# A four-layer attention/gated-MLP kernel: the first chunk's q and k from unpermuted weights, its softmax divided after the sum with v

## The chip, the cores and the metric

The kernel runs on one core of one Trainium2 chip. The time is what the device takes for one execution, in microseconds; of several runs the median counts. Engines are named as in the profile: PE is TensorE's matmul stream and PEld its weight loads, DVE is VectorE, ACT is ScalarE, POOL is GpSimd, SP is SyncE, whose queue issues all DMAs here.

## What is computed

Two kinds of layers alternate, A B A B, on 2048 tokens of width 576, each with a layer norm in front and a residual behind. A is attention with 32 heads of width 18, where each token looks at itself and at the tokens 2, 4, ... 14 before it. B is a gated product with 4608 hidden columns.

```python
def _A_ref(x, wqkv, wo):
    q, k, v = split_heads(x @ wqkv)                      # H = 32, Dh = 18
    off = jnp.arange(8) * 2
    idx = pos[:, None] - off[None, :]
    ...
    logits = jnp.einsum("bhsd,bhswd->bhsw", q, kg) * scale
    logits = jnp.where(mask[None, None, :, :], logits, -1e9)
    attn = _softmax(logits, axis=-1)
    o = jnp.einsum("bhsw,bhswd->bhsd", attn, vg)
    return o_joined @ wo

def _B_ref(x, w_gate, w_up, w_down):
    h = (x @ w_gate) * (x @ w_up)
    return h @ w_down

x = A_x
x = x + _A_ref(_layernorm(x, axis=-1), A_wqkv, A_wo)
x = x + _B_ref(_layernorm(x, axis=-1), B_w_gate, B_w_up, B_w_down)
x = x + _A_ref(_layernorm(x, axis=-1), A_wqkv, A_wo)
x = x + _B_ref(_layernorm(x, axis=-1), B_w_gate, B_w_up, B_w_down)
```

Both A layers use the same weights, and so do both B layers. `B_x` is not used.

## The kernel before

The tokens are cut into 16 tiles of 128. A chunk is one or two tiles: the first four chunks of the first layer pair are one tile each, the others two. For each chunk `attention` (L439) runs a layer A and `glu` (L768) a layer B. The list `seq` (L876) takes eight tiles through the first pair, then through the second, then the other eight.

No engine's order is written by hand. Every step is handed to `Plan.op` (L34) with its engine, a cost in nanoseconds, the keys that it reads and writes, and a priority; `Plan.run` (L70) then plays the steps against clocks of its own and emits them in that order, so each engine's queue is fixed when the program is built. `after=` adds an order without a data dependency, `hold`/`free` hand out PSUM banks, and `pair`/`need` the two "units" (a gate bank `pg` and an up bank `pu` each) that gate/up matmuls and projections share. While TensorE would idle before the first gate/up matmul, `warm` (L757) fills in matmuls of the identity.

All activations are kept transposed, features on partitions. For attention the 576 features of q, k and v are stored in the order (d, h), so that one partition block of 32 is one d for all heads: four full blocks of 128 and a tail of 64. The weights lie in DRAM as (h, d); so `setup_a` (L272) loads the raw rows into `wraw`, four blocks of 128 rows and the last 64 rows twice (both partition halves), 3456 bytes a row, and `setup_b` (L284) permutes their columns into `wqkv`: for each row block k, 512 columns of q and of v on VectorE (L305), of k on ScalarE (L307), and the last 192 columns on GpSimd (L303) or, for the last block, on VectorE. `wraw` lies in a pool that is given back (`swap`, L323), and the products' buffers are allocated in its place. SP's queue holds: two tiles of x, the six loads of `wraw`, two more tiles of x, eight loads of the output weights, then gate, up and down weights in slices.

The first chunk (`fast`, j = 0) is special. `head` (L353) normalizes the tile (statistics on VectorE, rstd by Ln and Exp on ScalarE, scaling on ScalarE L375, transposition on TensorE L386, eviction on ScalarE L389). `project` (L458) then runs, for each row block k, all fourteen output blocks of q, k, v (L469), as weights arrive. Four VectorE products of q with k shifted by two window places each (L580) are summed over d by matmuls with the selector `Esel` (L596). Softmax: mask (L616), maximum (L636), subtraction (L619), Exp on ScalarE (L659), sum and reciprocal (L664, L667), scaling (L670). The weights, one row for each head and quarter of the tokens, are spread to all partitions by matmuls with `Bsel` (L680) and evicted by ScalarE and VectorE (L522, L520). Eight VectorE products with shifted v (L714) are summed by identity matmuls (L718, L719), evicted (L734, L736), and `tail_fast` (L394) runs the output projection with the residual as an identity matmul (L400, L405), the second normalization (L407 to L423), its transposition (L429) and eviction (L431), which the first gate/up matmul (L793) waits for. Later chunks run the same steps in the shadow of the gate/up/down matmuls; chunk 1's and chunk 2's attention is partly ahead of L793 in TensorE's queue. The last 14 columns of k and v of a chunk are kept in `halo_k`, `halo_v` for the next (L562, L453, L526).

Of the kernel before, what the change touches and what calls it, by code (L numbers as in the profile page):

```python
# [7 lines left out]
FP32 = mybir.dt.float32  # L8
# [12 lines left out]
class Plan:  # L21
# [38 lines left out]

    def also(self, o, keys):

        for k in keys:
            for p in list(self.wr.get(k, ())) + list(self.rd.get(k, ())):
                if p is not o and p not in o.deps and p not in o.order:
                    o.deps.add(p)
                    p.succ.append(o)
                    o.n += 1

    def run(self, slots):  # L70
# [5 lines left out]
        while cand:  # L76
# [36 lines left out]
            if o.eng == "PE" and self.warm is not None:  # L113
                if o is self.cool:
                    self.warm = None
                else:
                    self.warm(min(44, int(max(0, t - clock["PE"] - 100) / 100)))
# [22 lines left out]
def kernel(  # L140
# [58 lines left out]
    Bsel = sb("Bsel", [P, 4, 4, 32])  # L199
    xf = [sb(f"xf{i}", [P, NST, D], FP32) for i in range(NXS)]  # L200
# [7 lines left out]
    zs_t = sb("zs", [P, CH // 4], FP32)  # L208
    xn_ = [[sb(f"xn{a}{i}", [P, KT * P]) for i in range(2)] for a in range(2)]
# [19 lines left out]
    startup_pool = tc.tile_pool(name="startup", bufs=1)  # L229
    sp = startup_pool.__enter__()  # L230
    wraw = sp.tile([P, KT, 3 * D], BF16, name="wraw")
    late = {}

# [29 lines left out]
    def load_x(t0, nst):  # L263
        b, i0 = (t0 // 2) % 2, t0 % 2
        if t0 == 2:
            op("POOL", 80, lambda: nc.gpsimd.memset(xb[b][0:1, i0, 0:2], 0.0), r=["wq3_0"], w=[f"xb{b}_{i0}"])
# [5 lines left out]
    def setup_a():  # L272
# [6 lines left out]
        for k in range(KF):  # L279
            op("SP", 500, dma(wraw[:, k, :], A_wqkv[k * P:(k + 1) * P, :]), w=[f"wraw{k}"], nbytes=P * 3 * D * 2, prio=1)  # L280
        for r_ in (0, TL):
            op("SP", 500, dma(wraw[r_:r_ + TL, KF, :], A_wqkv[KF * P:D, :]), w=[f"wrawt{r_}"], nbytes=TL * 3 * D * 2, prio=1)

    def setup_b():  # L284
        def mk_zero():
            for t_ in qT_ + kT_ + vT_:
                nc.gpsimd.memset(t_[TL:P, KF, :], 0.0)
            for t_ in halo_k + halo_v:
                nc.gpsimd.memset(t_[:], 0.0)
        op("POOL", 1500, mk_zero, w=[f"{x}{t}{i}" for x in "qkv" for t in (4, "H") for i in range(2)] + [f"halo{x}{i}" for x in "kv" for i in range(n_al)])  # L290
        for k in range(KT):
            for t3 in (0, 1, 2, 3):
                if t3 < 3:
                    src = wraw[:, k, t3 * D:(t3 + 1) * D].rearrange("p (h d) -> p d h", h=H)[:, 0:16, :]
                    dst = wqkv[:, k, t3 * 512:(t3 + 1) * 512].rearrange("p (d h) -> p d h", h=H)
                    cost = (615, 1080)
                else:
                    src = wraw[:, k, :].rearrange("p (t h d) -> p t d h", t=3, h=H)[:, :, 16:18, :]
                    dst = wqkv[:, k, 3 * 512:3 * D].rearrange("p (t d h) -> p t d h", t=3, h=H)
                    cost = (280, 500)  # L300
                rk = [f"wraw{k}"] if k < KF else ["wrawt0", f"wrawt{TL}"]
                if t3 == 3 and k < KF:
                    op("POOL", 700, lambda dst=dst, src=src: nc.gpsimd.tensor_copy(dst, src), r=rk, w=[f"wq{t3}_{k}"], prio=2)  # L303
                elif t3 != 1:
                    op("DVE", cost[0], lambda dst=dst, src=src: nc.vector.tensor_copy(dst, src), r=rk, w=[f"wq{t3}_{k}"], prio=2)  # L305
                else:
                    op("ACT", cost[1], lambda dst=dst, src=src: nc.scalar.copy(dst, src), r=rk, w=[f"wq{t3}_{k}"], prio=2)  # L307

        def mk_sel():
            nc.gpsimd.memset(Esel[:], 0.0)  # L310
# [10 lines left out]
        op("POOL", 5000, mk_sel, w=["sel"])  # L321

        def swap():  # L323
            startup_pool.__exit__(None, None, None)
            rot = ctx.enter_context(tc.tile_pool(name="rot", bufs=1))
            late["prod"] = [rot.tile([P, 2, KT, CH], BF16, name=f"prod{i}") for i in range(2)]
            late["s1"] = rot.tile([P, 8 * CH], BF16, name="s1")
            late["Lt"] = rot.tile([P, 2 * CH], FP32, name="Lt")
            late["a_c"] = late["s1"][:, 0:2 * CH]
            late["ab"] = rot.tile([P, 4, 2 * CH], BF16, name="ab")  # L330
        op("POOL", 0, swap, r=[f"wq{t}_{k}" for t in range(4) for k in range(KT)],
           w=["prod0", "prod1", "s10", "s11", "s12", "s13", "Lt", "ab"])

# [9 lines left out]
    def setup_glu():  # L343
        fw = F // FS
        for s in range(FS):
            fs = slice(s * fw, (s + 1) * fw)
            for nm, dst, src in (("wg", wg, B_w_gate), ("wu", wu, B_w_up)):
                op("SP", 500, dma(dst[:, :, fs], src[0:KF * P, fs].rearrange("(k p) f -> p k f", p=P)),
                   w=[f"{nm}{s}"], nbytes=P * KF * fw * 2, prio=4 + s, after=marks["x"])
# [3 lines left out]
    def head(src, keys, nst, dst, key, prio, ab, on_pe, mg, first=None, then=None):  # L353

        mv, st, rstd, nmr, xn = mv_[ab], st_[ab], rstd_[ab], nmr_[ab], xn_[ab]
        for i in range(nst):
# [573 lines left out]
```

## Time and profile before

| | |
|---|---|
| Runs | 1080.16, 1080.99, 1083.73 us; median 1080.99 |
| The profiled execution | 1079.86 us, its span 1078.1 us |
| Granted TensorE clock | 1.000 of full speed |
| TensorE busy up to 32 us, and 400 to 600 us | 26.1 of 32, and 199.4 of 200 |
| DMA, mean of the span | 136 GB/s (146 MB) |
| First gate/up matmul (L793) starts | 32.66 us |
| Last qkv weight copied by GpSimd / VectorE | 11.1 / 13.4 us |

The span runs from the first to the last instruction; the time of the execution holds what lies around it as well. A busy TensorE in the table includes the filler matmuls. The profile is one execution, and a name such as `pg` stands for all its buffers. In the chain of waits each piece is what the next one waited for, so a stretch of it is a stretch of the kernel's time, while a busy engine beside it is not.

### The profile page before, as it was taken

How to read it: one execution, taken by the hardware profiler on the slowest of the kernel's cores; microseconds unless marked ns; L12 is line 12 of the kernel's file. 1: busy time of each engine (PE TensorE's matmuls, PEld its weight loads, DVE VectorE, ACT ScalarE, POOL GpSimd, SP SyncE). 2: the span in 40 equal slices, each digit the busy share in tenths (PEclk: the TensorE clock that was granted, in tenths of full speed). 3: DMA queues.
4: the chain of work that ended last, by engine and by line, in shares of the span. 5: the costliest groups of instructions: out<-in, count | busy, mean ns of one | idle time of the engine just before them, and what ended most of it. 6: DMA issues, size and time to landing. Idle time of an engine off the chain costs nothing.

```text
span 1078.1 us, 25413 instructions
## 1 busy us (share of the span) xinstructions
PE 1063.8 (99%) x10797; PEld 787.7 (73%) x10797; DVE 755.1 (70%) x1345; ACT 369.4 (34%) x756; POOL 8.8 (1%) x39
## 2 busy tenths in 40 slices
PE   8999999999999999999999999999999999999998
PEld 6788877777777777777777777777777777777775
DVE  7677987786959776685967778595876869472222
ACT  6544254332421544131242332423243332212121
POOL 3000000000000000000000000000000000000000
PEclk9999999999999999999999999999999999999999
DMA  9973774645263644435363734536353543534331
GB/s 278 342 208 92 208 175 122 169 105 138 79 169 105 153 115 108 126 112 150 109 170 97 162 93 121 134 84 170 89 153 91 127 116 106 157 112 112 101 110 56
DMA packets 155089, 146.16 MB, mean 136 GB/s; under 512 B 43104, under 2 KB 152672, under 8 KB 154976
## 3 DMA queue, kind: packets, MB, share of 16 engines
q1 hardware_dynamic: 154976, 144.55, 49.6%
q8 instruction: 84, 1.38, 0.5%
q14 instruction: 29, 0.24, 0.1%
HBM read 125.11 MB, written 10.88 MB: 126 GB/s over the span
## 4 chain that ended last, share of the span: by engine, by line
PE 95%; DMA 2%; DVE 2%; SPq 1%; issue 1%; ACT 0%; DVEq 0%; ACTq 0%
PE pg L793 24%; PE pu L793 23%; PE acc L832 23%; PE pg L804 7%; PE pg L469 5%; PE pu L469 4%; PE pa L746 4%; PE acct L834 3%; DMA wraw<-in_A_wqkv_dram 1%; DMA a_dram<-s 1%; DMA ab<-a_dram 1%; DVE h L816 0%; SPq L257 0%; DVE prod L714 0%; PE pa L680 0%
## 5 line engine op out<-in xcount | busy, mean ns | idle before, releaser
L816 DVE TENSOR_TENSOR h<-pu,g_sb 128x512 bf16<-128x512 f32 x288 | 196.3, 686 | 200.8 <-ACT g_sb L815 149.6
L815 ACT CAST g_sb<-pg 128x512 bf16<-128x512 f32 x288 | 168.2, 585 | 476.6 <-PE pu L804 391.3
L832 PE MATMUL acc<-wd,h 128*128 128x512 bf16 x1152 | 306.3, 380 | 0.0
L793 PE MATMUL pg<-xnT_B,wg 128*128 128x256 bf16 (+1 forms) x2592 | 300.8, 261 | 0.8 <-ACT xnT_B L431 0.8
L793 PE MATMUL pu<-xnT_B,wu 128*128 128x256 bf16 (+1 forms) x2592 | 299.3, 261 | 0.0
L793 PEld LDWEIGHTS <-wg 128*128 128x128 bf16 x2592 | 212.5, 98 | 61.2 <-issue 26.2
L793 PEld LDWEIGHTS <-wu 128*128 128x128 bf16 x2592 | 230.9, 98 | 23.3
L834 PE MATMUL acct<-wd,h 128*128 128x64 bf16 x1152 | 222.0, 193 | 0.0
L832 PEld LDWEIGHTS <-h 128*128 128x128 bf16 x1152 | 112.7, 98 | 117.9
L714 DVE TENSOR_TENSOR prod<-vT,ab 128x1280 bf16<-128x1280 bf16 (+1 forms) x127 | 92.9, 741 | 66.5 <-DMA ab<-a_dram 66.4
L469 PEld LDWEIGHTS <-wqkv 128*128 128x128 bf16 (+1 forms) x1260 | 95.4, 97 | 30.3 <-issue 16.1
L834 PEld LDWEIGHTS <-h 128*128 128x128 bf16 x1152 | 112.9, 98 | 2.2
L580 DVE TENSOR_TENSOR prod<-qT,kT 128x2560 bf16<-128x2560 bf16 (+1 forms) x72 | 95.5, 1331 | 1.0 <-ACT kT L522 0.4
L731 DVE TENSOR_TENSOR oT<-oT,prod 128x1280 bf16<-128x1280 bf16 (+1 forms) x119 | 90.8, 763 | 3.0
L804 PE MATMUL pu<-xnT_B,wgu_t 64*128 64x256 bf16 (+1 forms) x648 | 88.1, 260 | 0.0
L804 PE MATMUL pg<-xnT_B,wgu_t 64*128 64x256 bf16 (+1 forms) x648 | 88.0, 260 | 0.0
L469 PE MATMUL pg<-xnT_A,wqkv 128*128 128x256 bf16 (+3 forms) x650 | 79.7, 260 | 1.5 <-issue 0.9
L469 PE MATMUL pu<-xnT_A,wqkv 128*128 128x256 bf16 (+3 forms) x610 | 76.5, 262 | 2.6 <-DVE h L816 2.1
L804 PEld LDWEIGHTS <-wgu_t 64*128 64x128 bf16 x1296 | 47.0, 94 | 32.5 <-issue 27.8
L746 PE MATMUL pa<-wo_p,oT 128*128 128x288 bf16 x310 | 48.2, 286 | 0.1
L375 ACT ACTIVATE xn<-xf,nmr,rstd 128x576 bf16<-128x576 f32 x47 | 40.7, 866 | 8.8 <-DVE nmr L367 8.8
L584 DVE TENSOR_TENSOR prod<-prod 128x1024 bf16<-128x1024 bf16 (+1 forms) x64 | 41.1, 643 | 0.8
(117 smaller groups left out, 563.1 us busy)
## 6 DMA issues: line engine op xcount, KB each, us to landing
wd<-in_B_w_down_dram SPq DMA_DIRECT2D x324, 288.0 KB, 3.3
s_dram<-s SPq DMA_DIRECT2D x13, 512.0 KB, 3.7
prod<-s_dram SPq DMA_DIRECT2D x52, 128.0 KB, 2.9
ab<-a_dram SPq DMA_DIRECT2D x52, 128.0 KB, 2.7
wg<-in_B_w_gate_dram SPq DMA_DIRECT2D x6, 768.0 KB, 9.8
wu<-in_B_w_up_dram SPq DMA_DIRECT2D x6, 768.0 KB, 10.4
out_dram<-ob SPq DMA_DIRECT2D x8, 288.0 KB, 2.6
wraw<-in_A_wqkv_dram SPq DMA_DIRECT2D x4, 432.0 KB, 5.0
```

The costliest lines, as they stand in the source:

```text
L469: nc.tensor.matmul(bank(p_, u)[0:m, e * n:(e + 1) * n], lhsT=wqkv[r_, k, c0:c0 + m], rhs=xnT_A[r_, k, 0:n], start=start, stop=stop, skip_g ...
L580: nc.vector.tensor_tensor(late["prod"][p_ % 2][:, :, :, 0:n], q2, k2, op=ALU.mult)
L584: nc.vector.tensor_tensor(prod[:, :, 0:4:2, 0:n], prod[:, :, 0:4:2, 0:n], prod[:, :, 1:4:2, 0:n], op=ALU.add)
L714: nc.vector.tensor_tensor(js(dst), js(vT[:, :, o0:o0 + n]), abw, op=ALU.mult)
L731: op("DVE", 60 + 3 * n, lambda i_=i_: nc.vector.tensor_tensor(oT[:, :, 0:n], oT[:, :, 0:n], late["prod"][i_ % 2][:, 0, :, 0:n], op=ALU.add ...
L746: nc.tensor.matmul(b()[:, 0:HD], lhsT=oT[:, t, i * P:(i + 1) * P], rhs=wo_p[:, t, hh * HD:(hh + 1) * HD], start=(t == 0), stop=(t == KT - 1))
L793: nc.tensor.matmul(pt[:, e * n:(e + 1) * n], lhsT=w_[:, k, ft * P:(ft + 1) * P], rhs=xT[:, k, 0:n], start=(first and k == 0 and e == 0), s ...
L804: nc.tensor.matmul(ps[:, e * n:(e + 1) * n], lhsT=wgu_t[r_, ft * P:(ft + 1) * P], rhs=xT[r_, KF, 0:n], start=(first and e == 0), stop=not ...
L815: op("ACT", 590, lambda: nc.scalar.copy(g_sb[gs][:, 0:ul], pg[use["slot"]][:, 0:ul]), r=[f"wg_{j}_{u}"], w=[f"g{gs}"], prio=0)
L816: op("DVE", 690, lambda: nc.vector.tensor_tensor(hb[hs][:, 0:ul], pu[use["slot"]][:, 0:ul], g_sb[gs][:, 0:ul], op=ALU.mult), r=[f"wu_{j}_{ ...
L832: nc.tensor.matmul(acc[i][:], lhsT=lhs, rhs=wt[:, e % 2, 0:512], start=(ft == 0), stop=(ft == NFT - 1))
L834: nc.tensor.matmul(acct[:, i * TL:(i + 1) * TL], lhsT=lhs, rhs=wt[:, e % 2, 512:D], start=(ft == 0 and i == 0), stop=(ft == NFT - 1), skip ...
```

## The change

- **Loads.** `wraw` is no tile of its own any more: its row blocks are the upper columns (2304 to 4031) of the `wu` and `wg` tiles, whose weights for these columns come later (their loads now also wait for the last reader of the raw weights). The columns of q and k (1152) are loaded first, in six loads, then those of v (576) in six more. Since nothing is given back, `swap` goes, and the products' buffers are allocated at the start.
- **Projection of the first chunk.** q and k are projected from the raw weights, block by block as these arrive (`natural`, `natural_tails`), so that they come out in the order (h, d). The selector that sums over d is a new one, `Nsel`, which sums features of one head in that order. v is projected from the permuted weights behind it, and k's last 14 columns, which chunk 1 needs in the order (d, h), are projected again from the permuted weights (`halo_mm`, from a copy `xh` of the last 14 tokens).
- **Permuting.** The copies into `wqkv` are dealt out anew: VectorE takes q, one block of v and one of k; ScalarE four of v, one of k; GpSimd all blocks of 192 columns and three of k's 512. They are behind the first chunk's own steps where `behind` says so.
- **Softmax of the first chunk.** Exp writes bf16 weights that are not divided; they are spread at once. The sums' reciprocals are split into two bf16 parts (`zh`), spread by eight small matmuls into `zb`, and multiply the summed products as these are evicted (on VectorE, where before ScalarE and VectorE copied).
- **The rest.** The first tile is scaled on VectorE; the output projection of the first chunk is in two steps (four blocks, then the tail); its transposed result is evicted by ScalarE (three blocks) and VectorE (two); the statistics and the transposed tile of one-tile chunks have a slot each; some priorities, orders and evictions of chunks 1 to 3 differ; the filler matmuls write a free unit's bank instead of `pa`.

```diff
@@ tiles
+    Nsel = sb("Nsel", [P, KT, 32])
+    xh = sb("xh", [P, KT, HALO])
+    zh = sb("zh", [P, 2, P // 4])
+    zb = sb("zb", [P, P], FP32)
-    startup_pool = tc.tile_pool(name="startup", bufs=1)
-    sp = startup_pool.__enter__()
-    wraw = sp.tile([P, KT, 3 * D], BF16, name="wraw")
+    wr0 = F // 2
+    wraw = [(wu[:, k] if k < KF else wg[:, 0])[:, wr0:wr0 + 3 * D] for k in range(KT)]
...
@@ setup_a
-        for k in range(KF):
-            op("SP", 500, dma(wraw[:, k, :], A_wqkv[k * P:(k + 1) * P, :]), ...)
-        for r_ in (0, TL):
-            op("SP", 500, dma(wraw[r_:r_ + TL, KF, :], A_wqkv[KF * P:D, :]), ...)
+        for c, cols in enumerate((slice(0, 2 * D), slice(2 * D, 3 * D))):
+            for k in range(KT):
+                for r_, key in zip(rows_[k], rk_[c][k]):
+                    m = r_.stop - r_.start
+                    op("SP", 500, dma(wraw[k][r_, cols], A_wqkv[k * P:k * P + m, cols]), w=[key], ...)
+            if c == 0:
+                load_x(1, 1)
...
@@ setup_b
+        for k in range(KT):
+            perm("DVE", 0, k)
+        for k in range(KT):
+            perm("ACT" if k else "DVE", 2, k)
+        for k in range(KT):
+            perm("POOL", 3, k)
+        for k in range(KT):
+            perm(("DVE", "ACT")[k] if k < 2 else "POOL", 1, k)
...
@@ head
+            if fast:
+                op("DVE", 600, apply_d, r=[keys[i - io], f"mv{ab}{i}", f"rstd{ab}{i}"], w=[f"xn{ab}{i}"], prio=0)
...
@@ attention, first chunk
+            def natural(k):
+                for e in range(KF):
+                    for p_ in range(2):
+                        nc.tensor.matmul(bank(p_, ua)[:, e * n:(e + 1) * n], lhsT=wraw[k][:, p_ * D + e * P:p_ * D + (e + 1) * P], rhs=xA[:, k, :], ...)
+                for p_ in range(2):
+                    nc.tensor.matmul(bq()[:, p_ * n:(p_ + 1) * n], lhsT=wraw[k][:, 512 + p_ * 512:640 + p_ * 512], rhs=xA[:, k, :], ...)
...
+            def vfull(p_, e, c0):
+                for k in range(KF):
+                    nc.tensor.matmul(bank(p_, uv)[:, e * n:(e + 1) * n], lhsT=wqkv[:, k, c0:c0 + P], rhs=xA[:, k, :], ...)
...
+            op("ACT", 250, lambda: nc.scalar.copy(xh[:], xA[:, :, n - HALO:n]), r=xk, w=["xh"], prio=prio)
...
@@ attention, chunk 1
+            def halo_mm(e):
+                for k in range(KF):
+                    nc.tensor.matmul(bh()[:, e * HALO:(e + 1) * HALO], lhsT=wqkv[:, k, parts[e]:parts[e] + P], rhs=xh[:, k, :], ...)
...
@@ attention, sum over d
-                        nc.tensor.matmul(pav[32 * jj:32 * jj + 32, 2 * p_:2 * p_ + 2, :], lhsT=Esel[:],
+                        nc.tensor.matmul(pav[32 * jj:32 * jj + 32, 2 * p_:2 * p_ + 2, :], lhsT=Nsel[:, i_] if fast else Esel[:],
...
@@ attention, softmax
+        if fast:
+            marks["exp"] = op("ACT", 400, lambda: nc.scalar.activation(late["a_c"][:, 0:W * sq], late["Lt"][:, 0:W * sq], ACT.Exp), ...)
...
+                if fast and j0:
+                    pl.behind(marks["perms"]["ACT", 1, 1], ev)
+                    pl.behind(marks["perms"]["DVE", 1, 0], lastp)
...
+                op("DVE", 590, lambda: nc.vector.tensor_reduce(out=zs_t[:, 0:sq], in_=wv(late["a_c"]).rearrange("p w s -> p s w"), op=ALU.add, axis=AX.X), ...)
+                def invert():
+                    nc.vector.reciprocal(zs_t[:, 0:sq], zs_t[:, 0:sq])
+                    nc.vector.tensor_copy(zh[:, 0], zs_t[:, 0:sq])
+                    nc.vector.tensor_tensor(zh[:, 1], zs_t[:, 0:sq], zh[:, 0], op=ALU.subtract)
+                def zspread():
+                    for jj in range(4):
+                        for i in range(2):
+                            nc.tensor.matmul(bz()[:, jj * sq:(jj + 1) * sq], lhsT=Bsel[:, jj].rearrange("p a b -> p (a b)"), rhs=zh[:, i], ...)
...
@@ attention, eviction of the sum with v
-            op("ACT", 590, lambda: nc.scalar.copy(oT[:, 0:KF, 0:n], bo[0]()[:, 0:KF * n].rearrange("p (k s) -> p k s", k=KF)), ...)
-            op("DVE", 200, lambda: nc.vector.tensor_copy(oT[:, KF, 0:n], bo[1]()[:, 0:n]), ...)
+            op("DVE", 690, lambda: nc.vector.tensor_tensor(oT[:, 0:KF, 0:n], bo[0]()[:, 0:KF * n].rearrange("p (k s) -> p k s", k=KF),
+                                                           zb[:].unsqueeze(1).to_broadcast([P, KF, n]), op=ALU.mult), ...)
+            op("DVE", 270, lambda: nc.vector.tensor_tensor(oT[:, KF, 0:n], bo[1]()[:, 0:n], zb[:], op=ALU.mult), ...)
```

In the changed kernel's queues this gives the following order. SP: two tiles of x, the six loads of q and k, four blocks of v and half of the last, two more tiles of x, the other half, the output weights, then the slices. VectorE, after the first statistics: the scaled tile, q's five copies with chunk 1's statistics between them, one copy of v, the two evictions of k, the four products, one copy of k, mask, maximum, subtraction, chunk 2's statistics, the sums, the eviction of half the weights, the reciprocal and its two parts, the eight products with v. ScalarE, after the evictions of q: four copies of v, chunk 1's scaling, Exp, the evictions of v, half the weights. GpSimd: the selectors, the zeros, one 512-column copy, five of 192, two of 512. TensorE: the matmuls of q and k, 27 fillers, three sums over d, eight matmuls of v, the fourth sum, the rest of v.

355 lines of the change are left out of this document (223 added, 132 removed).

## The prediction

> **What bounds the kernel now.** I read the page's table of engines first: TensorE is busy for 99% of the span, so after its start the kernel can only be as short as its matmuls.
>
> ```profile
> PE 1063.8 (99%) x10797; PEld 787.7 (73%) x10797; DVE 755.1 (70%) x1345; ACT 369.4 (34%) x756; POOL 8.8 (1%) x39
> ```
>
> Then TensorE's waits from 100 to 1073 us: one line of 2.1 us in four waits. With a pause of 0.85 us at 40.8 us (timeline) that is all TensorE loses once the first gate/up matmul (L793) has started at 32.66 us. The change touches what comes before.
>
> ```profile
> PE pu L469 <- DVE h L816: 2.1, 4, 0.5
> ```
>
> So I read the chain of waits from 0 to 34 us in order of time (start, length, what).
>
> ```profile
> 4.35 7.37 DMA wraw<-in_A_wqkv_dram
> ...
> 11.81 1.56 DVE wqkv L305 x3
> ...
> 14.83 0.89 DVE prod L580 x2
> ...
> 18.30 0.28 DVE acct L616
> ...
> 19.58 0.43 ACT Lt L659
> 20.03 0.60 DVE zs L664
> 20.66 0.36 DVE zs L667
> 21.05 0.43 DVE s L670
> ...
> 26.87 0.89 PE pg L469 x16
> 27.77 0.12 PE acc L400
> 27.89 0.61 PE acct L405 x5
> 28.50 0.63 PE acc L405 x5
> ...
> 32.66 1.05 PE pg L793 x16
> ```
>
> The chain waits for the last rows of the qkv weights until 11.72 us, then runs through three permuting copies, the products of q and k, the softmax, the products with v, the output projection and the second normalization. What the change is worth is how far it moves the 32.66. Two more views price its parts: the stretches of 2 us (PE, PEld, DVE, ACT, POOL busy, clock, DMA share, GB/s) and the copies into `wqkv` between 8.2 and 9 us (min/median/max ns).
>
> ```profile
> 6.00:8.00 2.00, 1.74 (x26) 1.62 (x24) 2.00 (x5) 2.00 (x4) 1.59 (x11) 1.00 0.99 392
> ...
> 10.00:12.00 2.00, 1.76 (x25) 1.19 (x22) 1.71 (x4) 1.33 (x2) 0.99 (x1) 1.00 1.09 246
> ```
>
> ```profile
> L305 DVE COPY wqkv<-wraw x2: 619/790/961, 8.0 to 8.5; 128x512 bf16<-128x512 bf16 x2
> L303 POOL COPY wqkv<-wraw x1: 1016/1016/1016, 8.0 to 8.0; 128x192 bf16<-128x192 bf16 x1
> ```
>
> **The change, part by part.** Times are along that chain.
>
> *Loads.* All 576 rows of 3456 bytes (1.99 MB) are ahead of the gate; then only the 2304 bytes of q and k are (1.33 MB), 0.66 MB less. The stretches from 4 to 12 us moved 349, 392, 272 and 246 GB/s, on average 315: 2.1 us, so the gate falls from 11.7 to 9.6. At 246 GB/s, the rate as the last rows came in, it would be 2.7 us; the other end is zero, if a packet costs the same at any length, as there are as many rows. I take 2.1, since the rate rises and falls with the bytes over these stretches: **-2.1**. SP issues six more loads, each about 0.43 us; the v loads stand behind those of q and k, and the first gate weights, which landed at 18.5 us, have some ten microseconds to spare.
>
> *From the gate to the first product.* Before: 14.83 - 11.72 = 3.1 us. TensorE can now use the raw weights, but VectorE's queue still has two copies (q's last rows, v's first) of 0.62 and a small operation of 0.15 ahead of its evictions of k (0.69 and 0.29, the rows at 13.41 and 14.13 us); with five gaps of 0.04, 2.6 us. TensorE's last ten matmuls (about 0.85 us with their drain) and ScalarE's evictions of q (0.60 and 0.27) lie beside it: 1.7 us. **-0.5**.
>
> *Products and logits.* The four products take 3.0 us as before. Behind the last one stands a copy of 0.62, where VectorE waited 0.43 us for TensorE (17.87 to 18.30): **+0.2**. The fourth sum on TensorE now stands behind eight v matmuls that wait for ScalarE's copies; three copies of 1.12 from about 11.4 us end at 14.8, before the fourth product at 15.2, so nothing. The exponential on ScalarE is queued behind four such copies and a normalization (0.87 + 0.42): 9.6 + 0.85 + 0.87 + 4.5 + 1.3 + 0.2 of gaps = 17.3, where VectorE has the logits at 17.1: **+0.2**.
>
> *Softmax without the division.* Exponential's end to the first product with v was 20.0 to 22.95, 2.95 us. Now the sums (0.59), an eviction of half the weights (0.69), the reciprocal (0.35) and two small operations (0.15 each, as the nmr row) follow each other on VectorE: 2.0. ScalarE's v evictions (0.59, 0.26) and its half of the weights (0.59) fit beside them. **-0.95**. One small VectorE operation of 0.15 now stands among the eight products with v: **+0.15**. Spreading the reciprocals (eight small matmuls, one ScalarE copy) lies under these products (3.3 us); uncovered it would be some 0.6.
>
> *From the last product with v to the gate/up start.* Before: 26.25 to 32.66, 6.4 us. TensorE's queue now has all of chunk 1's sixteen projection matmuls (0.89, as before) and its fourteen tails (24.73 to 25.28: 0.55) ahead of the output projection, so statistics come 0.55 later; the scaled eviction on VectorE (0.69 where ScalarE took 0.57) is ready sooner than that. Behind the normalization VectorE has two statistics (0.45 each) and their aggregate (0.2) ahead of its part of the transposed tile: 0.83 + 0.9 + 0.2 + 0.34 = 2.3 from rstd, where the chain had 2.2: 0.1. The 25 halo matmuls, priced between a 128x64 one (0.03 in the chain) and a 128x128 one (0.056), 0.7 to 1.4 us, replace sixteen filler matmuls (0.9) and an idle 0.7: I add 0.15. **+0.8**.
>
> Sum: -2.1 - 0.5 + 0.2 + 0.2 - 0.95 + 0.15 + 0.8 = -2.2 us.
>
> *GpSimd's copies.* Before, GpSimd copied four blocks of 192 columns; now five, and three of 512. The VectorE copy that ran while GpSimd copied took 0.96 (three such: 1.07, 0.96, 0.96), its neighbours 0.62: 0.35 for each meeting, and 0.35 x 512/192 = 0.93 for a large one. Two or three small copies and one large one meet the stretch from the gate to the logits: 3 x 0.35 + 0.93 = 2.0 us, if products of q and k suffer as copies do. No product runs beside GpSimd in this trace, so the other end is zero; I take the middle, **+1.0**, as nothing favours an end. [...]
>
> TensorE's matmuls after the start are the same; their order differs here and there, so the five pauses (0.85 + 2.1 = 2.9 us) may go or double. I take no change. Loads of later weights come about as before and are used a microsecond earlier; the tightest, the second slice's tails, landed at 28.9 and were used at 34.9.
>
> All told -1.2 us. The profiled run took 1079.86 us (span 1078.1), so 1078.7 for one like it; the median of the runs shown is 1.1 above it, so I forecast **1079.8**, its own range 1078 to 1082.
>
> **The rivals.**
> *More is gained.* The loads come at the 2.7 end, the products do not suffer from GpSimd and half the later pauses go: -2.2 - 0.6 - 1.45 = -4.25, 1076.7 us. For it: the gate is one block on the chain; against: it needs three good ends at once.
> *The gate does not move.* Rows, not bytes, set the loads: -1.2 + 2.1 = +0.9, 1081.9. For it: 2304-byte rows are no fewer, and the last 64-row loads came slowly; against: the GB/s of the stretches varies widely.
> *Slower: GpSimd takes VectorE's time.* Every one of the eight copies holds VectorE for its own length alone, 0.51 for a small one (the row at 6.19 us), 0.51 x 512/192 = 1.36 for a large: 5 x 0.51 + 3 x 1.36 = 6.6 us, less 0.9 that falls into VectorE's waits for loads: -2.2 + 5.7 = +3.5, 1084.5. The gain is gone from 2.2 us of such holds on; from 5.4 on the kernel is slower by 0.3%. For it: all three slow copies stand beside a GpSimd copy; against: each lost 0.35 to 0.45, not 0.51, and evictions from PSUM may not meet. [...]
>
> **Chances.** Forecast 0.45, more gained 0.32, gate unmoved 0.11, slower 0.12. 0.3% (3.2 us) is about what a measurement of this kernel can tell from no change: faster 0.32, same 0.56, slower 0.12. The range, 1075.5 to 1083.5, reaches to the case of more gained and over that of the unmoved gate.
>
> **What would show it.** In the changed kernel's profile: the last q,k weight landing near 9.6; the first product of q and k 2.6 after it; its four products 3.0 long, or longer by 0.35 or more beside each GpSimd copy; 2.0 from exponential to products with v; the first gate/up matmul near 31.5. It is wrong if that matmul starts before 29.5 or after 33, or if TensorE's pauses after it differ by more than 3 us.

## The result, and the profile after

The changed kernel takes 1084.43 us (median of 20 runs, 1082.97 to 1088.01), the kernel before 1081.8 beside it (20 runs, 1080.03 to 1085.2): ratio 1.0025, 95% interval 1.0017 to 1.0034. A small loss, where a gain of 1.2 us was forecast; the time lies outside the range. The profiled run took 1084.29 us with a span of 1082.6, 4.5 more than the profiled run of before, which was one of the quickest of its kernel.

TensorE is still the bound. First the line of engines, then TensorE's waits after 100 us (what waits, what ended it; us in total, times, longest):

```profile
PE 1058.3 (98%) x10663; PEld 789.9 (73%) x10819; DVE 760.2 (70%) x1349; ACT 365.3 (34%) x751; POOL 15.4 (1%) x46
```

```profile
PE pu L510 <- DVE h L961: 2.7, 5, 0.9
PE pa L891 <- DVE xf L897: 0.5, 2, 0.2
```

Then the chain of waits of the changed kernel from 0 to 36 us (start, length, what):

```profile
3.16 5.74 DMA wu<-in_A_wqkv_dram
...
10.97 0.96 DVE wqkv L346
11.93 0.42 DVE nmr L395
...
13.38 0.89 DVE prod L694 x2
...
16.85 1.74 DVE prod L694
18.63 0.46 PE acc L710 x16
19.09 0.97 PE pg L622 x8
...
21.88 0.42 PE acct L800 x2
...
33.37 0.74 DVE st L385 x2
34.12 0.21 DVE mv L387
34.33 0.17 DVE xnT_B L468
34.52 0.49 ACT xnT_B L467
35.05 1.00 PE pg L938 x15
```

The last line is the first gate/up matmul: 35.05 us instead of 32.66, where 31.5 was forecast. Stage by stage, from the instructions of the two traces:

| stage | before | after |
|---|---|---|
| last q, k weight landed | 11.72 | 10.26 |
| to the first product of q and k | 3.11 | 3.12 |
| four products | 3.03 | 5.19 |
| to the end of the exponential | 2.14 | 2.21 |
| to the first product with v | 2.95 | 3.30 |
| eight products with v | 3.30 | 3.36 |
| to the first gate/up matmul | 6.41 | 7.61 |
| first gate/up matmul | 32.66 | 35.05 |
| from there to the end of the span | 1045.4 | 1047.5 |

So, against this profile of the kernel before, 2.4 us are lost ahead of the start and 2.1 behind it. A second profile of the kernel before, below, starts at 35.34, so that the first part differs from run to run. Two views show what happened ahead of the start. The four products on VectorE as one group (min/median/max ns, first and last start), and the timeline of GpSimd (start, length, what):

```profile
L694 DVE TENSOR_TENSOR prod<-qT,kT x4: 826/1438/1726, 13.4 to 16.8; 128x1280 bf16<-128x1280 bf16 x4
```

```profile
10.50 2.76 POOL L346 COPY wqkv<-wu 128x192 bf16<-128x192 bf16 x4 [1.04 <-DMA wu<-in_A_wqkv_dram]
13.74 0.85 POOL L346 COPY wqkv<-wg 128x192 bf16<-128x192 bf16 x1 [0.48 <-DMA wg<-in_A_wqkv_dram]
14.54 1.70 POOL L346 COPY wqkv<-wu 128x512 bf16<-128x512 bf16 x1
16.19 1.70 POOL L346 COPY wqkv<-wg 128x512 bf16<-128x512 bf16 x1
```

The first large copy ends at 16.24 and the third product at 16.92; the second copy at 17.89 and the fourth product at 18.57: each product ends 0.68 after the copy that it met, and the second copy ends 0.97 after the third product: the ends of the two engines alternate. And in the stretches of 2 us (PE, PEld, DVE, ACT, POOL busy, then the granted clock):

```profile
12.00:14.00 2.00, 0.37 (x7) 0.29 (x5) 1.86 (x4) 2.00 (x3) 1.52 (x4) 1.00 0.66 187
14.00:16.00 2.00, 1.04 (x43) 0.80 (x43) 2.00 (x3) 2.00 (x3) 2.00 (x2) 1.00 0.85 186
16.00:18.00 2.00, 1.02 (x28) 0.79 (x27) 2.00 (x2) 0.94 (x2) 1.89 (x2) 0.87 0.72 191
18.00:20.00 2.00, 1.46 (x31) 1.38 (x31) 1.90 (x5) 0.00 (x0) 0.00 (x0) 0.50 1.06 400
20.00:22.00 2.00, 2.00 (x19) 1.54 (x17) 1.71 (x5) 1.26 (x3) 0.00 (x0) 0.50 1.08 346
```

TensorE is busy for 0.37 us of 12 to 14 and, waiting for the slow products, for half of 14 to 18 us; then the granted clock is 0.5, in the trace from 17.48 to 24.31 us. The v projection behind the exponential's sums runs at half speed (0.12 us a matmul of 128x128 in the chain above, 0.97 for 8; 0.056 in the same trace from 28.30 us on, at clock 1.0, 0.89 for 16), and the spread (L800), released by the exponential at 20.78, starts at 21.88.

### The profile page after: what moved, and what is told of

Read it like the earlier page. It is cut to its first block, busy times and chain, and to the rows that moved or that the text cites. A ratio compares the mean times of both kernels' runs of the same rounds, so it can differ in the third digit from the quotient of the medians.

```text
span 1082.6 us, 25316 instructions
## 1 busy us (share of the span) xinstructions
PE 1058.3 (98%) x10663; PEld 789.9 (73%) x10819; DVE 760.2 (70%) x1349; ACT 365.3 (34%) x751; POOL 15.4 (1%) x46
## 3 DMA queue, kind: packets, MB, share of 16 engines
q8 instruction: 84, 1.38, 0.5%
## 4 chain that ended last, share of the span: by engine, by line
PE 91%; DVE 5%; DMA 2%; issue 2%; SPq 0%; ACT 0%; DVEq 0%
PE pg L938 23%; PE pu L938 22%; PE acc L977 19%; PE pg L949 7%; PE pg L510 5%; PE acct L979 5%; PE pu L510 4%; PE pa L891 3%; DVE prod L857 1%; DVE h L961 1%; DVE oT L874 1%; DMA ab<-a_dram 1%; DMA a_dram<-s 1%; DVE prod L694 1%; DMA wu<-in_A_wqkv_dram 1%
## 5 line engine op out<-in xcount | busy, mean ns | idle before, releaser
L977 PE MATMUL acc<-wd,h 128*128 128x512 bf16 x996 | 286.2, 380 | 0.0
L510 PEld LDWEIGHTS <-wqkv 128*128 128x128 bf16 (+1 forms) x1190 | 91.7, 97 | 27.3 <-issue 14.6
L694 DVE TENSOR_TENSOR prod<-qT,kT 128x2560 bf16<-128x2560 bf16 (+1 forms) x72 | 97.7, 1361 | 0.7 <-ACT kT L550 0.4
L510 PE MATMUL pg<-xnT_A,wqkv 128*128 128x256 bf16 (+3 forms) x610 | 75.8, 263 | 0.0
L510 PE MATMUL pu<-xnT_A,wqkv 128*128 128x256 bf16 (+3 forms) x580 | 73.1, 264 | 2.7 <-DVE h L961 2.7
```

Of the source, the lines that this page charges most:

```text
L510: nc.tensor.matmul(bank(p_, u)[0:m, e * n:(e + 1) * n], lhsT=wqkv[r_, k, c0:c0 + m], rhs=xA[r_, k, :], start=start, stop=stop, skip_group_ ...
L694: nc.vector.tensor_tensor(late["prod"][p_ % 2][:, :, :, 0:n], q2, k2, op=ALU.mult)
L977: nc.tensor.matmul(acc[i][:], lhsT=lhs, rhs=wt[:, e % 2, 0:512], start=(ft == 0), stop=(ft == NFT - 1))
```

## The experiments

Times are medians; "above" is against runs of the kernel before taken beside them, ratios with their 95% interval. "Start" is the first gate/up matmul of the profiled run, "rest" what its span has behind it.

**GpSimd beside VectorE.** To the kernel before, three GpSimd copies were added that nothing reads:

```
+ op("POOL", 10, lambda: nc.gpsimd.tensor_copy(tick[0:TL], kT[0:TL, KF, HALO:HALO + 2]), r=qk, w=["tick"])
+ for _ in range(3): op("POOL", 10, <copy of 128x512 from wqkv to spare>, r=["tick"], w=["spare"])
```

> The kernel before with three additional GpSimd copies of 512 columns into a scratch tile that nothing reads, released by the last eviction of k, so that they run beside the four q.k products. Theory A (GpSimd's copies slow VectorE's products): the four products take about 5 us instead of 3.03, each product beside a copy 1.5 to 1.8 us instead of 0.75 to 0.83, time about 2.0 above the kernel before, near 1083.8, and about 1 more if the clock falls too. Rival B (the products of the changed kernel are slow because of something else in it): products 3.0 us, time within 0.3 of the kernel before.

1085.94, ratio 1.0044 (1.0031 to 1.0057), 4.5 above; start 37.82, rest 1045.8. GpSimd's copies and the products on VectorE:

```profile
14.29 4.37 POOL L569 COPY spare<-wqkv 128x512 bf16<-128x512 bf16 x3
```

```profile
L586 DVE TENSOR_TENSOR prod<-qT,kT x4: 812/1632/1718, 14.5 to 19.3; 128x1280 bf16<-128x1280 bf16 x4
```

Three products take 1.55 to 1.72 and each ends 0.68 or 0.69 behind a copy; the fourth, alone, takes 0.81. The four last 5.56 us. Theory A holds, with the clock's share: it stands at 0.5 for 10.2 us. The inverse, in the changed kernel:

```
+ held = op("POOL", 60, <2-column copy that reads the last product>, r=[pk], w=["tick"])
+ for k in (2, 3, 4): pl.behind(marks["perms"]["POOL", 1, k], held)
  # and the planner's cost of these copies: 2500 -> 1500
```

> The changed kernel with GpSimd's three 512-column weight copies held back until the last of the four q.k products is written (a two-column copy that reads that product stands ahead of them in GpSimd's queue); the five 192-column copies stay where they are. Theory A (the four products take 5.19 us instead of 3.03 because GpSimd copies beside them): products back to 3.0 to 3.3 us, the sums on TensorE come closer together, the granted clock stays at 1.0 between 17 and 24 us, the exponential's end to the first v product falls from 3.30 to about 2.3; first gate/up matmul at 32.0 to 32.7 instead of 35.05, time near 1081.7 (2.7 below the changed kernel's 1084.4). Rival B (the products are slow for a reason of their own, such as the layout that the unpermuted weights give): products stay at 5.2, time 1084.4. Rival C (contention and clock are separate): products short, clock still 0.5, time near 1082.5.

The products take 0.83, 0.82, 1.15 and 0.81, the start is 31.97: the cause of the slow products is GpSimd. Of the 3.1 us by which the start is earlier, the products give 1.8; 0.9 lie ahead of the first product, where the loads landed 0.8 earlier. Two of the numbers missed: the clock still fell for 3.4 us, and the time is 1084.82, ratio 1.0035 (1.0023 to 1.0047), no better. A start 3.1 us earlier brought nothing; the rest is 1051.2. TensorE's waits of this run between 35 and 70 us ("issue" means that the profile shows nothing that it waited for):

```profile
PE pa L711 <- issue: 1.5, 1, 1.5
PE acc L981 <- DMA wd<-in_B_w_down_dram: 1.4, 1, 1.4
PE pu L942 <- issue: 0.6, 1, 0.6
```

The second line is a down-projection weight that lands at 65.02 us; the same load of the kernel before lands at 63.53, and its TensorE, coming later, waits for none of them. Part of an early start is given back here.

**The clock.** More filler matmuls in the changed kernel (62, 10, 12 ahead of the sums):

```
- self.warm(min(44, m), slot)
+ self.warm(2 * m + 8 if m and 9000 < clock["PE"] < 16000 else min(44, m), slot)
```

> The changed kernel with more filler matmuls on TensorE ahead of the first three sums of the q.k products (62, 10, 12 instead of 27, 1, 2); nothing else differs. Theory A (the clock falls to 0.5 from 17.5 to 24.3 us because TensorE idles between the sums, and this costs the spread and v's projection about 1.0 us): clock 1.0 throughout, exponential's end to first v product 3.30 to about 2.3 us, the four products still 5.2 us; first gate/up matmul near 34.0, time about 1.0 below the changed kernel, near 1083.4. Rival B (the clock falls for another reason, or v's path is set by ScalarE and VectorE and not by TensorE): time within 0.3 of the changed kernel.

The clock stays at 1.0 and the exponential's end to the first product with v falls to 2.18, as theory A has it. The start is 33.12, 1.9 earlier, of which 0.8 lie ahead of the first product, after loads that landed 1.2 earlier. But the time is 1083.9, ratio 1.0021 (1.0011 to 1.0031), hardly better than the changed kernel's 1.0025, with a rest of 1048.2 and 4.2 us of waits for h. The same idea in the kernel before (36, 4, 6, 4, 27, 19 fillers):

> The kernel before with more filler matmuls around the four sums of the q.k products and the spread (36, 4, 6, 4, 27, 19 instead of 21, 1, 2, 1, 15, 10); nothing else differs. Of the last 16 runs of the kernel before, those with a granted clock of 1.000 lie at 1079.7 to 1081.9 and those at 0.996 to 0.999 at 1081.1 to 1084.6. Theory A (the clock also falls in the start of the kernel before, in about half of its runs, for the same idling of TensorE): every run at clock 1.000, median 1080.3 to 1081.0. Rival B (the clock does not hang on the fillers, or what the slower runs lose is not the clock): median within 0.4 of the kernel before and clocks below 1.000 in half of the runs.

Both theories missed: 1085.75, ratio 1.0031 (1.0020 to 1.0042). The start was 33.31; the rest 1051.3, with waits for h of 4.9 us and the clock at half once, from 703 us on.

**The tail.** Statistics of a later chunk behind the eviction of the transposed tile in the changed kernel, `{3: "nmr"}` replaced by a mark on that eviction:

> The changed kernel with the statistics of a later chunk's x tile (two of 0.45 us and one of 0.21 on VectorE) ordered behind VectorE's half of the eviction of the transposed tile, which they preceded; nothing else moves ahead of the gate/up start. Theory A (of the 1.2 us by which the tail grew about half is VectorE's half eviction standing behind these statistics, with ScalarE's half waiting for it): last transpose to first gate/up matmul falls from about 1.3 to 0.8 us, first gate/up matmul at 34.5 instead of 35.05, time 0.5 below the changed kernel, near 1083.9. Rival B (ScalarE's half is held by its own queue, or the start waits for weights): start at 35.0, time within 0.2 of the changed kernel.

1084.57, ratio 1.0033 (1.0020 to 1.0046): rival B. The last product with v to the start fell from 7.61 to 7.41, not by 0.55.

**The planner's order.** One number that moves its model of the start, in the changed kernel and in the kernel before:

```
  if o is self.cool:
      self.warm = None
+     t += 4600        # kernel before: 2400
```

> The changed kernel with one number of the planner changed: in its model of time the first gate/up matmul starts 4.6 us later (at 35.05, where the trace has it, instead of 30.45), so that everything before it is issued as in the changed kernel and only the order of what follows is planned anew. Theory A (a part of the loss, +2.1 us between the first gate/up matmul and the end in the two profiles, is an order of the later work planned for a start that the chip does not reach): first gate/up matmul unchanged near 35, the pauses after it fall from 4.85 us towards the 3.15 of the kernel before, time 1 to 2 below the changed kernel, 1082.5 to 1083.5. Rival B (the later pauses come from the late start itself, or from loads, and not from the order): time within 0.4 of the changed kernel's 1084.4.

> The kernel before with the same number of the planner moved by 2.4 us (first gate/up matmul planned at 35.26 instead of 32.86; the trace has 32.66): nothing changes ahead of the start, the order behind it is planned for a start that is 2.6 us away from the real one. Theory A (an order planned for another start costs time by itself): first gate/up matmul near 32.7 as before, later pauses up from 3.15 to 4 to 6 us, time 1 to 2.5 above the kernel before, 1082.5 to 1084. Rival B (the order does not matter): time within 0.4 of the kernel before's 1081.6.

1084.62, ratio 1.0029 (1.0018 to 1.0039), rest 1048.3: the first is rival B. 1083.24, ratio 1.0009 (1.0000 to 1.0018), rest 1046.9: between the theories; its profile has the clock at half for 6.8 us and so a start of 34.80, and its waits behind 200 us are those of the kernel before. An order planned for the right start, which differs up to 67 us behind it only, is not what the changed kernel lacks.

**All three edits together** (held copies, fillers, planned start + 1300):

> The changed kernel with three edits together: GpSimd's three 512-column copies held until the last q.k product, the filler matmuls of the second experiment (62, 10, 12), and the planner told a first gate/up matmul at 31.75 us instead of 30.45. If GpSimd's contention, the clock and the planned order are the three causes: products 3.0 to 3.4 us, clock 1.0 throughout, first gate/up matmul at 31.0 to 31.6, after it some pauses because the down-projection weights land at 65 us in every run so far (about 2 us of the earlier start given back there), later pauses as in the kernel before; time 1079.5 to 1081.5, that is not above the kernel before's 1081.6. Rival (the order of the later work is not the cause, or the weights take all of it): time 1083.5 to 1084.8, like the first experiment.

1089.13, ratio 1.0065 (1.0052 to 1.0079): start 31.52, products 3.37, clock 1.0 there, all as wanted, and the slowest so far. TensorE waits 3.5 us for weights between 50 and 66 us; the longest, 2.4 us, is followed by 3.4 us at half clock.

**More room for the round trip**: `3500` replaced by `5500` in the margin of the products with v.

> The kernel before with one number of the planner changed: from the seventh chunk on (j 6 and up) it counts 5.5 us instead of 3.5 us for the attention weights to come back through DRAM, so that more of VectorE's other work (the products h of gate and up) is ordered ahead of the first product with v, which waits for them. The start is untouched. Theory A (the pauses of TensorE at 390, 573, 697 and 821 us, which wait for h, are VectorE standing in its queue behind a round trip that lands late): these pauses (2.2 us in the profile of the kernel before) vanish, time 1.5 to 2.5 below the kernel before, 1079.2 to 1080.3. Rival B (the wait only moves to the next use): time within 0.5 of the kernel before.

> The changed kernel with the same 5.5 for 3.5. Theory A: the pauses that wait for h between 390 and 830 us (2.8 us in its profile) vanish, time 1081.5 to 1082.5, and what is left between it and the kernel before with 5.5 is the late start alone, 2.4 to 2.9. Rival B (the later loss of the changed kernel is not these pauses): time within 0.5 of 1084.4.

> The changed kernel with 5.5 for 3.5 and with the filler matmuls 62, 10, 12 of the second experiment. Theory A (without the later pauses the end follows the start): first gate/up matmul near 33.1, clock 1.0, time 1.5 to 2.0 below the changed kernel with 5.5 alone, 0.4 to 0.9 above the kernel before with 5.5: near 1080.2. Rival B (the end does not follow the start even then): time within 0.6 of the changed kernel with 5.5 alone, as the second experiment was within 0.6 of the changed kernel.

> The changed kernel with 5.5 for 3.5, the fillers, and GpSimd's three 512-column copies held until the last q.k product. First gate/up matmul at 31.0 to 32.0. Theory A (a start before some 32.7 us is given back, because the down-projection weights land at 65 us in every kernel and TensorE then waits for them, as in the first experiment): waits for loads of 1 to 3 us between 50 and 68 us, time equal to or up to 1.5 above the fillers' kernel with 5.5. Rival B (the start passes on to the end): time 1.0 to 1.6 below the fillers' kernel with 5.5, near 1079, below both kernels.

None of the expected times was met: 1088.1, 1089.82, 1086.61 and 1088.63 (ratios 1.0067, 1.0079, 1.0042 and 1.0062, the lowest interval 1.0029 to 1.0055). The waits for h did not vanish but moved, as rival B has it, from 390, 573, 697 and 821 us to 647, 712, 778, 844 and 909. These four say little on the start, since their order of the later work is another; in the third the clock fell for 3.4 us in spite of the fillers, and the last again waits for weights, as its theory A has it, 5.0 us between 46 and 67 us, from a start of 31.54.

**A late start and nothing else.** Fillers ahead of the first gate/up matmul of the kernel before:

```
  if o is self.cool:
+     self.warm(25)    # 36, 58
      self.warm = None
```

> The kernel before, unchanged, for a second profile and as the zero of the three runs beside it. Its first profile (1079.86) lies 1.8 under the median of its runs (1081.6). Theory A (the slower of its runs lose it in the start, where the clock falls): a profile near 1081.6 or slower shows a clock below 1.0 between 15 and 25 us and the first gate/up matmul later than 32.66. Theory B (they lose it later): first gate/up matmul within 0.5 of 32.66, and pauses behind h between 200 and 900 us of more than the 2.2 us of the first profile.

> The kernel before with 25 filler matmuls (55 ns each) ahead of its first gate/up matmul: 14 of them lie in the wait that is there, 11 delay the start by about 0.5 us. Nothing else changes. Theory A (a late start passes on to the end one to one): time 0.5 above the kernel before. Theory B (what a start is worth hangs on how the later round trips of the attention weights through DRAM fall among the weight loads, by more than on the start itself): the times of the three delays are not in the order of the delays, or differ from them by more than 1 us, as the eighth experiment did (start 0.65 later, time 3.7 above).

> The kernel before with 36 filler matmuls ahead of its first gate/up matmul, a delay of about 1.1 us. Theory A: time 1.1 above the kernel before. Theory B: off that by more than 1 us.

> The kernel before with 58 filler matmuls ahead of its first gate/up matmul, a delay of about 2.3 us, as large as the changed kernel's (2.4 in the profiles). Theory A: time 2.3 above the kernel before, that is the whole of the changed kernel's loss (2.6 of the medians) follows from its late start. Theory B: off that by more than 1 us.

The unchanged kernel's second profile (1082.35) starts at 35.34, its clock at half from 18.96 to 25.79, with a rest of 1045.2: theory A. Its start is 2.7 us late, 0.6 by the loads (12.31 instead of 11.72) and 2.1 by the clock, and this passes on one to one. The three delays, planned as 0.5, 1.1 and 2.3, are 2.7, 3.6 and 2.4 above (1.0024, 1.0030 and 1.0023; the lower ends 1.0014 or more): not in their order, and theory B for the first two; the third alone has theory A's number. Where the first lost it, VectorE and then TensorE near 392 us (start, length, what, the wait before it):

```profile
391.91 0.82 DVE L715 TENSOR_TENSOR prod<-vT,ab 128x1280 bf16<-128x1280 bf16 x1 [8.05 <-DMA ab<-a_dram]
```

```profile
393.39 0.73 PE L470 MATMUL pu<-xnT_A,wqkv 128*128 128x256 bf16 x4 [2.05 <-DVE h L817]
```

And the same product in the first profile of the kernel before:

```profile
387.34 0.83 DVE L714 TENSOR_TENSOR prod<-vT,ab 128x1280 bf16<-128x1280 bf16 x1 [5.63 <-DMA ab<-a_dram]
```

The attention weights come back from DRAM later, h stands behind the products with v in VectorE's queue, and TensorE's next projection waits for h. The order is the same in both; only when the transfer lands differs: the last of its four reads takes 4.9 us in the delayed run and 2.7 in the kernel before. The clock then stands at half from 393.7 to 397.1.

**The number of instructions.** The delays had added instructions; the late starts that passed on one to one had not. So the rows of TensorE's program ahead of the first gate/up matmul were to be varied alone (a matmul and its weight load are two). The DMA view of the kernel before shows how the program comes in:

```profile
q8 instruction: 84, 1.38, 0.5%
```

84 transfers of 16 KB for TensorE's 21594 rows, one per 257 rows; from the start of one to the start of the next TensorE gets on by 255 rows in the mean (253 in the changed kernel), and so they are read as its program. In the kernel before, 25 fillers were put where TensorE idles; in the changed kernel the clock was held by few long fillers (128x512) so that 799 rows lie ahead as in the kernel before:

```
+ self.warm(m + 25 if m > 18 and clock["PE"] > 9000 else min(44, m))   # kernel before
+ self.long(15 if m > 20 else 3, slot)                                 # changed kernel, ahead of the sums
+ self.long(5, slot); self.warm(4, slot)                               # and behind the spread
```

> The kernel before with 25 filler matmuls more between q and k's projections and the first sum of products, where TensorE idles for 2 us (46 instead of 21): no work is delayed, but TensorE's program ahead of the first gate/up matmul grows from 799 to 849 rows, exactly as in the run with the 0.5 us delay. TensorE's program comes in by DMA about every 14 us (84 loads of 16 KB for 21600 rows, 256 rows each), among the same transfers as the attention weights' round trips. Theory A (the later losses hang on where these program loads fall in the work, and a different number of instructions ahead moves them all): first gate/up matmul within 0.5 of 32.66 or, where the clock falls, of 35.3, but pauses of more than 1 us at 390 to 395 us and of 0.2 to 0.5 near 227 to 231 us as in the run with the 0.5 us delay, time 1.5 to 3 above the kernel before. Theory B (the later losses come from a late start on TensorE alone, out of step with the other engines): time within 0.4 of the kernel before, or below it by the clock.

> The changed kernel with the clock held up by fillers of 512 columns (15, 3, 3 ahead of the sums, 5 behind the spread) in place of the many of 128 columns, so that TensorE's program ahead of the first gate/up matmul has 799 rows as in the kernel before (changed kernel 843, second experiment 951). First gate/up matmul near 33.1, clock 1.0. Theory A (place of the program loads): later losses of at most 0.7 us instead of the 2.3 of the second experiment; time 1080.5 to 1082.0, that is about the kernel before's. Theory B (the order of the later work or the phase): time near the second experiment's 1083.9, 2.0 or more above the kernel before.

The first is 1.4 above, ratio 1.0017 (1.0006 to 1.0028), between the theories. It is not free of a delay, as was meant: the 46 fillers end at 16.7 us, the first sum stands behind them, the third product waits 0.39 us for the sum, and the four products take 3.51 us instead of 3.03. TensorE's waits behind 100 us:

```profile
PE pu L470 <- DVE h L817: 3.0, 6, 0.7
PE pu L794 <- DVE h L817: 0.6, 1, 0.6
PE pa L747 <- DVE xf L753: 0.5, 2, 0.2
```

The last line is the pair of waits (0.23 each at 227 and 229 us) that the delayed run has too and the kernel before has not; the one near 393 us is 0.7, not 2.3. Over all runs this pair is in each of the eight profiles with 843 to 871 rows ahead, from starts of 31.97 to 35.84, and in none of the six with 799. The second, the changed kernel in place, is 1082.02, ratio 1.0003 (0.9993 to 1.0013): theory A's time, and no difference from the kernel before that can be measured. Start 34.09, clock 1.0, rest 1046.2, with the waits:

```profile
PE pu L517 <- DVE h L973: 1.6, 4, 0.5
PE pg L950 <- ACT g_sb L972: 0.6, 1, 0.6
```

Its order behind the start is that of the second experiment, its rest 2.0 shorter. All runs but those with other margins, by the rows ahead:

| rows | kernel | start | rest | late part | above |
|---|---|---|---|---|---|
| 799 | before, first and second profile | 32.66, 35.34 | 1045.4, 1045.2 | none | 0 |
| 799 | before + GpSimd copies | 37.82 | 1045.8 | none | 4.5 |
| 799 | changed, in place | 34.09 | 1046.2 | none | 0.4 |
| 799 | before, planned anew | 34.80 | 1046.9 | none | 1.2 |
| 843 | changed; tail; planned anew | 35.05; 35.55; 35.15 | 1047.5; 1047.7; 1048.3 | 1.01; 1.25; 1.34 | 2.6; 3.1; 2.5 |
| 849 | before + 25 fillers, early; ahead of the start | 33.42; 33.86 | 1048.3; 1050.5 | 0.93; 2.21, 1.00 | 1.4; 2.7 |
| 871, 915 | before, longer delays | 35.20; 35.23 | 1048.1; 1046.4 | 0.97, 1.03; 0.51 | 3.6; 2.4 |
| 891 | before + fillers | 33.31 | 1051.3 | 0.61, 1.56 | 3.7 |
| 951 | changed + fillers | 33.12 | 1048.2 | 1.26, 1.15 | 2.4 |
| 843, 951 | changed, early starts | 31.97; 31.52 | 1051.2; 1055.9 | 1.18; 1.38, 0.72, 1.15 | 3.4; 7.0 |

With 799 rows the rest is 1045.2 to 1046.9; with any other number 1046.4 to 1051.3, and from a start before 32 us 1051 or more. That rows put back take most of the loss away is one kernel's result; rows moved without any delay were not run.

The traces show how rows can act. Each read of the attention weights lands in 16 parts. In the delayed run 15 parts of the last read have landed at 389.62 us and the sixteenth at 391.83; a program transfer of 16 KB had begun at 388.63 and took 1.98 us. Over the 20 traces, 272 of the 1040 reads have such a transfer of TensorE's program under way: in 43 of these the last part is more than 1 us behind the one before it, and in none of the other 768. The column "late part" gives this distance, in us and from 0.5 on, for the four round trips (a write and its reads) ahead of the waits near 390, 573, 697 and 821 us: there is none with 799 rows, and at least one with any other number. Since the transfers follow the rows (one every 255 and 253 in the two kernels), rows added ahead of the start move them against the round trips. Elsewhere (262, 500 and 935 us in the kernel before, with 1.38, 1.47 and 1.57 us) a late part cost no wait. That the late parts are all of the difference in the rest is not shown.

## Why the prediction was wrong, point by point

- *Loads, -2.1*: right. 10.26 against 11.72 is -1.5, but these landings vary: over ten profiles with each way of loading they are 11.42 to 12.89 and 9.08 to 10.28, the middles 2.2 apart.
- *Gate to first product, -0.5*: zero. The last copy of VectorE took 0.96 instead of 0.62 and the small operation 0.50 instead of 0.15, both beside GpSimd's small copies: the GpSimd term began here.
- *GpSimd's copies, +1.0*: **this step failed.** Its prices were right: a meeting with a small copy cost 0.34, 0.35 and 0.33 (forecast 0.35), one with a large copy 0.90 and 0.91 (0.93). Wrong were the middle of 0 and 2.0, taken because the trace of before had no product beside a copy, and the count, since two large copies met the products and not one. The products alone lost 2.2, and the 0.5 above went the same way: 2.7, beyond the upper end. Undone, it brings the start to 31.97 but not the time (1084.82); so it is not the whole. The rival "GpSimd takes VectorE's time" had what the traces show, that a product beside a copy does not end before it (0.68 or 0.69 us behind the copy's end, in three kernels), and its 1084.5 is the measured time by luck: it put 5.7 into VectorE, and the rest came from elsewhere.
- *The clock* was in no step. It was read as 1.00 in the kernel before, and nothing was asked of what slower products do to TensorE. The softmax's -0.95 became +0.35 through it; with the clock held it is 2.18 against 2.95, -0.8: that step was right. Slow products are not needed for the fall: the kernel before has it in its second profile with products of 3.03.
- *Copy behind the products +0.2, exponential +0.2, small operation +0.15*: the first two together 0.07, the third 0.06. *Tail, +0.8*: 1.2; moving the two statistics gave back 0.2, the rest was not taken apart.
- *"I take no change" behind the start* failed second: +2.1 in the profiles. The bound was named (the pauses may go or double), its cause was not; the late parts above are at least some of it. In place, with the clock held, 1.3 of it goes, and the start is 1.0 earlier; the two are the 2.3 by which that kernel beats the changed one against the kernel before.
- Even the forecast start of 31.5 was no gain where it was reached: two kernels, with 951 rows ahead, waited 3.5 and 5.0 us for weights. "Loads of later weights ... are used a microsecond earlier" looked at the second slice; the last ones, at 65 us, were the tight ones.
- The kernel before was priced by a profile with the clock at 1.0 throughout; its second one, at 0.997, starts as late as the changed kernel. Of 103 runs of the kernel before beside the experiments 34 have a granted clock of 1.000 (median 1080.7) and 24 one of 0.997 or less (1083.2); of the changed kernel's 20 none has 1.000, and 17 have 0.997 or less (1084.5). At a like clock the changed kernel is thus 1.3 us slower; the other half of the loss goes with a clock that falls in nearly every run instead of in some.

## What to carry to other kernels

Work moved to an idle engine is priced by whom it meets, instruction by instruction, and then by what the engine that waits for these does in the meantime: here GpSimd slowed VectorE (four products took 5.19 us instead of 3.03), and the clock of TensorE, idle for half of 14 to 18 us meanwhile, fell to 0.5 from 17.48 to 24.31 us; none of the 20 runs has a granted clock of 1.000. Before a start is bought, look for the transfer that is nearly late behind it, and for program transfers that fall into a round trip (43 of 272 reads that had one under way were more than 1 us late in their last part). When an edit adds or removes instructions, run it also with the same number of filler instructions and no change of work, and see in the trace that they delay nothing, or differences such as the 0.17 to 0.31% that fillers alone made in five runs of the kernel before will be put down to the edit.

## What had not been expected of the hardware

A product of 0.82 us on VectorE ended 0.68 us after the GpSimd copy that it met and so took up to 1.73 us; a copy (0.96 instead of 0.62) and even a 128x1 operation (0.50 instead of 0.15) were lengthened too, and so was GpSimd's copy, 1.70 us beside products and 1.09 in the held run. Not all were: in the held run the operations on the logits in PSUM (0.27, 0.42 and 0.42) and the statistics (0.45 and 0.44) kept their lengths beside the three copies. The granted clock stood at half for 3.4 us (the held run), 6.8 (the changed kernel, and the second profile of the kernel before) or 10.2 (the run with GpSimd's added copies), that is one, two or three times 3.41, also at 66, 394, 397 and 703 us behind pauses of 1.3 to 2.4; other pauses of this size, up to the 1.68 at 47.6 us of the run with GpSimd's added copies, had no fall behind them. The same program had the fall ahead of the start in one profile (18.96 to 25.79 us) and not in the other; what decides is not shown. A transfer of TensorE's program, 16 KB, took 1.0 us in the median of the kernel before and 1.98 in the delayed run, where the read beside it landed late; over all traces it went with a last part more than 1 us late in 43 of 272 reads.
